# Attention reads and a cosine router in one kernel: the last seven expert blocks moved behind two run-time branches

## The chip, the cores and the metric

The kernel runs on one core of one Trainium2 chip. The metric is device time in microseconds (us) of one execution, median of the runs; all data is float32.

## What is computed

The reference has two parts. The first reads a batch of rows against a small set of states, both ways; the second sends every resulting row to the one expert whose embedding it resembles most.

```python
def _attn_ref(x, state):               # x (8, 8, 512, 64), state (8, 8, 32, 64)
    scores = scale * np.matmul(x, state.transpose(0, 1, 3, 2))
    ...
    xread = np.matmul(a, state)        # a: softmax of scores
    ...
    sread = np.matmul(a2, x)           # a2: softmax of scores the other way
    return np.concatenate([xread, sread], axis=2)

def _moe_ref(x, expert_emb, tau, w1, w2):   # x (4352, 512), 8 experts, F = 1024
    logits = xn @ en.T / tau                # xn, en: x and expert_emb by their lengths
    expert_idx = np.argmax(logits, axis=1)
    ...
    for e in range(E):
        mask = expert_idx == e
        ...
        h = np.maximum(x[mask] @ w1[e], 0.0)
        out[mask] = gate_w[mask, None] * (h @ w2[e])
```

The 8 x (512 + 32) = 4352 rows are 34 x 128. The inputs come from a fixed seed, so how many rows each expert gets is the same in every run.

## The kernel before

The work has three stages, one behind the other.

**First part (lines 89 to 344).** For each of 8 batches and 2 groups of heads TensorE computes scores and reads. Rows go to a buffer in DRAM, x_rows. Meanwhile SyncE's queue loads the first weights of all eight experts into SBUF, where they stay (w1_sb, 16 MB).

**The seam (lines 346 to 441).** The kernel puts the rows in blocks of 128 rows of one expert. An expert with n rows takes n / 128 blocks, rounded up; nb holds these numbers and b0 each expert's first block. With 4352 rows and 8 experts there are at least 34 blocks and at most 34 + 7 = 41 (NBLK). VectorE makes one-hot matrices (bm, oh, and rr with the row numbers; GpSimd makes the half of rr with the gates), and 34 matmuls (inv_ps, line 427) turn them into src_row and dst_row: which row stands at each place of each block, and where its result goes. An empty place reads row 0 and gets a destination past the end of the output, so that nothing is written for it. eblk is each block's expert.

**Second part, the expert stage (lines 443 to 542).** All 41 blocks run, whatever the counts are. A block j has these steps: `gather(j)`, an indirect DMA issued by GpSimd that fetches its 128 rows (xin, three buffers); `load_w2(j)`, a 2 MB load of the expert's second weights issued by SyncE (w2, two buffers); `turn_x`, four transposes on TensorE (xt_ps) and a copy on VectorE (xT); `hidden`, 8 matmuls against w1_sb (h_ps), with ReLU on ScalarE and VectorE; `turn_h`, eight transposes (ht_ps) and two copies (hT); `result`, 8 matmuls against w2 (y_ps), a multiplication by the gate on VectorE (y), and an indirect DMA on GpSimd that scatters the rows to the output. The profile counts two passes for each float32 matmul, hence 16 records for each of the two big steps. SyncE and TensorE read the block's expert into a register first (`expert`, line 446, a TENSOR_LOAD).

The order of the work is that of the loop, on each engine's own queue. It runs ahead: the hidden layer of the next block, the gather three blocks ahead, the second weights two blocks ahead.

```python
528    xin = {j: gather(j) for j in range(3)}
529    w2 = {j: load_w2(j) for j in range(2)}
530    xT = {j: turn_x(xin.pop(j)) for j in range(2)}
531    h = {0: hidden(0, xT.pop(0))}
532    for j in range(NBLK):
533        if j + 1 < NBLK:
534            h[j + 1] = hidden(j + 1, xT.pop(j + 1))
535        hT = turn_h(h.pop(j))
536        if j + 3 < NBLK:
537            xin[j + 3] = gather(j + 3)
538        if j + 2 < NBLK:
539            xT[j + 2] = turn_x(xin.pop(j + 2))
540        result(j, hT, w2.pop(j))
541        if j + 2 < NBLK:
542            w2[j + 2] = load_w2(j + 2)
```

In what follows h(j), y(j) and w2(j) are block j's hidden step, result step and second weights; blocks count from 0.

Of the kernel before, what the change touches and what calls it, by code (L numbers as in the profile page):

```python
# [10 lines left out]
I32 = mybir.dt.int32  # L11
AF = mybir.ActivationFunctionType
ALU = mybir.AluOpType
AX = mybir.AxisListType.X
PSUM = bass.MemoryType.PSUM
ROUND = 12582912.0  # 1.5 * 2**23: adding and subtracting it rounds to a whole number


@with_exitstack
def kernel(  # L20
# [10 lines left out]
    nc = tc.nc  # L31
    P = 128
# [4 lines left out]
    N = out.shape[0]  # L37
    R = S + Ns  # rows of one batch in the second part
    NCH = S // P  # row p * NCH + c of a batch sits in partition p, chunk c
    HG = 2  # groups of heads  # L40
    HPG = H // HG  # heads in a group: HPG * Ns = 128 rows of states
    GW = HPG * Dh  # features of a group
    XW = GW + E  # and the group's share of the logits behind them
    KD = D // P
    KF = F // P
    SCALE = float(Dh) ** -0.5
    NG = 2  # groups of batches: NCH slots a batch, and one for the group's state rows
    GB = B // NG
    SG = GB * NCH + 1
    NSLOT = NG * SG  # L50
    NBLK = N // P + E - 1  # blocks of 128 rows of one expert, at most
    BIG = 200000.0
# [37 lines left out]
    dst_row = pers.tile([P, NBLK], I32, name="dst_row")  # L90
    eblk = pers.tile([1, NBLK], I32, name="eblk")

    make_identity(nc, ident)

# [1 line left out]
    with ExitStack() as att_ctx:  # L96
# [24 lines left out]

        # Block diagonals of states, with the projections on the experts behind each group's.
        bdst = [att1.tile([P, HG, XW], FP32, name=f"bdst{i}") for i in range(2)]
        for t in bdst:
            nc.gpsimd.memset(t, 0.0)

        # Experts by their length and by tau, features in partitions.
        junk8 = att1.tile([P, D], FP32, tag="junk", name="junk8")[0:E]
# [11 lines left out]

        # What the routing needs that rests on shapes alone.
        nc.gpsimd.memset(ones, 1.0)
# [22 lines left out]
        def choose(s0, ns):  # L165
            """One-hot of each row's first greatest logit, and the counts of the slots before."""
            l = lg[:, s0 : s0 + ns]
            mx = lmax[:, s0 : s0 + ns]
            shp = [P, ns, E]
            sel = att1.tile([P, NCH, E], FP32, tag="sel", name="sel")[:, 0:ns]  # L170
            pm = att1.tile([P, NCH], FP32, tag="pm", name="pm")[:, 0:ns]
            nc.vector.tensor_reduce(mx.unsqueeze(2), l, axis=AX, op=ALU.max)
            nc.vector.tensor_tensor(sel, l, bc(mx, shp, 2), ALU.is_equal)
            nc.vector.tensor_tensor(sel, sel, bc(pref, shp, 1), ALU.mult)
            nc.vector.tensor_reduce(pm.unsqueeze(2), sel, axis=AX, op=ALU.max)
            nc.vector.tensor_tensor(eq[:, s0 : s0 + ns], sel, bc(pm, shp, 2), ALU.is_equal)
            for s in range(s0, s0 + ns):
                nc.gpsimd.tensor_tensor(cumx[:, s + 1], cumx[:, s], eq[:, s], ALU.add)

        def states(b):  # L180
            """The batch's states as block diagonals, as they are and transposed."""
            bs = bdst[b % 2]
            for i in range(HPG):
                nc.gpsimd.tensor_copy(
                    bs[Ns * i : Ns * i + Ns, :, Dh * i : Dh * i + Dh], st_nat[Ns * i : Ns * i + Ns, b]
                )
            ps = bank("st_ps")
            for g in range(HG):
                for j in range(2):
                    nc.tensor.transpose(  # L190
                        ps[:, (2 * g + j) * P : (2 * g + j + 1) * P], bs[:, g, j * P : j * P + P], ident
                    )
            bd = att.tile([P, HG, 2, P], FP32, tag="bd", name="bd")
            nc.scalar.activation(bd.rearrange("p g j n -> p (g j n)"), ps, AF.Copy)
            pp = bank("pj_ps")
            for g in range(HG):
                for j in range(2):
                    nc.tensor.matmul(  # L198
                        pp[:, g * E : g * E + E], lhsT=bd[:, g, j], rhs=enT[:, 2 * g + j],
                        start=(j == 0), stop=(j == 1),  # L200
                    )
            nc.vector.tensor_copy(
                bs[:, :, GW:XW], pp[:, 0 : HG * E].rearrange("p (g e) -> p g e", e=E)
            )
            return bs, bd

        def scores(b, g, xn, bd):
            """Scores of a group of heads both ways, and their exponentials."""
            xT = att.tile([P, 2, S], FP32, tag="xT", name="xT")
# [11 lines left out]
            for j in range(2):  # L221
                for c in range(NCH):
# [5 lines left out]
                    )  # L228
            # Over the rows: a state's scores lie in its partition.
            r2 = att.tile([P, 3], FP32, tag="r2", name="r2")  # L230
# [7 lines left out]
            nc.vector.tensor_scalar(dg, ident, r2[:, 2:3], None, ALU.mult)  # L238
            # Over the states of a head.
            nch = NCH * HPG  # L240
# [13 lines left out]
        def reads(b, g, xn, bs, xr, e1, e2, dg):  # L254
            """A group's columns of the batch's rows."""
            ps = bank("a_ps")
# [29 lines left out]
        def rows(b, xr):  # L286
            """Keep the batch's rows, and say where they go."""
            s0 = SG * (b // GB) + NCH * (b % GB)
            for g in range(HG):
                nc.sync.dma_start(  # L290
                    rows_by_batch[b, 0:S, g * GW : g * GW + GW].rearrange("(p c) d -> p c d", c=NCH),
                    xr[:, :, g, 0:GW],
                )
            nc.vector.tensor_tensor(lg[:, s0 : s0 + NCH], xr[:, :, 0, GW:XW], xr[:, :, 1, GW:XW], ALU.add)
            junk = att1.tile([P, D], FP32, tag="junk", name="junk")
            for c in range(NCH):
                nc.scalar.activation(
                    junk.rearrange("p (g d) -> p g d", g=HG), xr[:, c, :, 0:GW], AF.Square, accum_out=ssq[:, s0 + c : s0 + c + 1]
                )
            choose(s0, NCH)  # L300

        def state_rows(g):
            """The same for the states read in a group of batches."""
            s0 = SG * g + SG - 1
# [40 lines left out]

# [1 line left out]
    with tc.tile_pool(name="rt", bufs=1) as rt:  # L347
# [3 lines left out]

        # Gates: the greatest probability of each row.
        shp = [P, NSLOT, E]
# [11 lines left out]

        # A row's rank among its expert's, and the experts' counts behind them.
        nk = NSLOT * E
# [10 lines left out]
        def whole(dst, src, shift):  # L378
            """src / 128 up (shift > 0) or down to a whole number, of whole numbers src."""
            nc.vector.tensor_scalar(dst, src, 1.0 / P, shift, ALU.mult, ALU.add)  # L380
            nc.vector.tensor_scalar(dst, dst, ROUND, ROUND, ALU.add, ALU.subtract)

# [21 lines left out]

        # A block's expert: the last one that starts no later.
        shp = [1, NBLK, E]
# [5 lines left out]

        # Which row, with which gate, stands at each place of each block.
        shp = [P, NSLOT, NBLK]
# [19 lines left out]
        nc.vector.tensor_copy(gpos, inv[:, 1])  # L434
        # An empty place reads row 0, and is written nowhere.
        nc.vector.tensor_scalar(src_row, inv[:, 0], -1.0, 0.0, ALU.add, ALU.max)
# [4 lines left out]

# [1 line left out]
    moe = ctx.enter_context(tc.tile_pool(name="moe", bufs=2))  # L443
# [10 lines left out]
    def load_w2(j):  # L454
        t = moe.tile([P, KF, D], FP32, tag="w2", name="w2")
        ek = expert(j, mybir.EngineType.SP)
        nc.sync.dma_start(t, moe_w2[ds(ek, 1)].rearrange("o (k p) d -> p (o k) d", p=P))
        return t
# [68 lines left out]

    xin = {j: gather(j) for j in range(3)}
    w2 = {j: load_w2(j) for j in range(2)}
    xT = {j: turn_x(xin.pop(j)) for j in range(2)}  # L530
    h = {0: hidden(0, xT.pop(0))}
    for j in range(NBLK):
        if j + 1 < NBLK:
            h[j + 1] = hidden(j + 1, xT.pop(j + 1))
        hT = turn_h(h.pop(j))
        if j + 3 < NBLK:
            xin[j + 3] = gather(j + 3)
        if j + 2 < NBLK:
            xT[j + 2] = turn_x(xin.pop(j + 2))
        result(j, hT, w2.pop(j))  # L540
        if j + 2 < NBLK:
            w2[j + 2] = load_w2(j + 2)

# [29 lines left out]
```

## Time and profile before

| what | us |
|---|---|
| three timed runs | 885.47, 887.55, 893.33 |
| their median | 887.55 |
| profiled execution, first to last instruction (span) | 891.5 |

The span of the profiled execution lies between the timed runs; no device time of its own is listed for it. PE is TensorE's matmuls, PEld its weight loads, DVE is VectorE, ACT ScalarE, POOL GpSimd, SP SyncE; SPq and POOLq are the queues of the last two. L512 is line 512 of the kernel before. Times in the rows are us from the start of the span, unless marked ns.

### The profile page before, as it was taken

How to read it: one execution, taken by the hardware profiler on the slowest of the kernel's cores; microseconds unless marked ns; L12 is line 12 of the kernel's file. 1: busy time of each engine (PE TensorE's matmuls, PEld its weight loads, DVE VectorE, ACT ScalarE, POOL GpSimd, SP SyncE). 2: the span in 40 equal slices, each digit the busy share in tenths (PEclk: the TensorE clock that was granted, in tenths of full speed). 3: DMA queues.
4: the chain of work that ended last, by engine and by line, in shares of the span. 5: the costliest groups of instructions: out<-in, count | busy, mean ns of one | idle time of the engine just before them, and what ended most of it. 6: DMA issues, size and time to landing. Idle time of an engine off the chain costs nothing.

```text
span 891.5 us, 8858 instructions
## 1 busy us (share of the span) xinstructions
PE 830.0 (93%) x3280; PEld 467.8 (52%) x3280; DVE 234.2 (26%) x514; ACT 138.5 (16%) x280; POOL 125.0 (14%) x192
## 2 busy tenths in 40 slices
PE   6899999995659999999999999999999999999995
PEld 4677777774624444454545454444444454545442
DVE  3454556546211112121212121211111121212110
ACT  3343444443001000000000010101000000000000
POOL 2111111110120111111111111111111111110000
PEclk9899999997569999999999999999999999999998
DMA  9486844311073454555545464636464545545340
GB/s 269 156 285 189 260 130 95 72 49 60 0 248 103 144 195 159 176 178 161 193 149 198 136 207 132 215 132 219 134 204 145 186 168 171 174 154 188 123 163 0
DMA packets 97553, 140.84 MB, mean 158 GB/s; under 512 B 38174, under 2 KB 46366, under 8 KB 97512
## 3 DMA queue, kind: packets, MB, share of 16 engines
q1 hardware_dynamic: 90920, 120.59, 41.9%
q0 software_dynamic: 6560, 19.67, 6.6%
q8 instruction: 27, 0.44, 0.2%
q14 instruction: 14, 0.11, 0.0%
q10 hardware_dynamic: 32, 0.02, 0.0%
HBM read 122.44 MB, written 19.66 MB: 159 GB/s over the span
## 4 chain that ended last, share of the span: by engine, by line
issue 62%; PE 20%; POOL 10%; DVE 5%; DMA 2%; POOLq 1%; ACT 1%; DVEq 0%
PE sT_ps L218 5%; POOL out_dram L517 4%; POOL xin L462 4%; PE s_ps L223 3%; PE x_ps L270 3%; PE sr_ps L278 3%; PE inv_ps L427 2%; PE e_ps L263 1%; DVE xT L70 1%; PE pj_ps L198 1%; DMA xin<-x_rows,src_row 1%; PE a_ps L258 1%; DMA x_rows<-xs 1%; PE xt_ps L214 1%; PE st_ps L190 1%
## 5 line engine op out<-in xcount | busy, mean ns | idle before, releaser
L512 PE MATMUL y_ps<-w,hT 128*128 128x512 f32 x656 | 292.4, 599 | 0.6 <-ACT hT L68 0.6
L486 PE MATMUL h_ps<-w_sb,xT 128*128 x656 | 289.4, 594 | 0.0
L486 PEld LDWEIGHTS h_ps<-w_sb,xT 128*128 128x128 f32 x656 | 125.1, 191 | 157.3 <-issue 157.2
L512 PEld LDWEIGHTS y_ps<-w,hT 128*128 128x128 f32 x656 | 121.3, 190 | 142.2 <-issue 137.3
L494 ACT ACTIVATE h<-h_ps 128x512 f32<-128x512 f32 x41 | 24.5, 597 | 467.6 <-PE h_ps L486 467.6
L516 DVE TENSOR_SCALAR y<-y_ps,gpos 128x512 f32<-128x512 f32 x41 | 30.8, 751 | 250.6 <-PE y_ps L512 250.6
L496 DVE TENSOR_SCALAR h<-h_ps 128x512 f32<-128x512 f32 x41 | 28.4, 692 | 254.4 <-PE h_ps L486 254.4
L517 POOL DMA_INDIRECT out_dram<-y,dst_row x41 | 41.6, 1015 | 307.5 <-DVE y L516 307.5
L462 POOL DMA_INDIRECT xin<-x_rows,src_row x41 | 42.2, 1030 | 261.0 <-PE xt_ps L475 237.8
L505 PEld LDWEIGHTS ht_ps<-ident,h 128*128 128x128 f32 x328 | 38.3, 140 | 21.6 <-issue 21.6
L218 PE MATMUL sT_ps<-xT,bd 128*128 128x512 f32 x64 | 40.9, 772 | 7.4 <-DVE xT L70 7.2
L68 ACT ACTIVATE hT<-ht_ps 128x512 f32<-128x512 f32 x41 | 24.5, 597 | 138.6 <-PE ht_ps L505 138.6
L505 PE MATMUL ht_ps<-ident,h 128*128 128x128 f32 x328 | 42.5, 272 | 0.0
L223 PEld LDWEIGHTS s_ps<-bd,xT 128*128 128x128 f32 x256 | 33.1, 200 | 11.1 <-issue 11.1
L475 PE MATMUL xt_ps<-ident,xin 128*128 128x128 f32 x164 | 25.6, 280 | 9.9 <-DMA xin<-x_rows,src_row 9.9
L270 PE MATMUL x_ps<-bdst,aT 128*128 128x264 f32 x128 | 33.4, 405 | 0.0
L278 PEld LDWEIGHTS sr_ps<-xn,a 128*32 128x32 f32 x512 | 29.0, 110 | 5.5 <-DVE r L248 4.5
L278 PE MATMUL sr_ps<-xn,a 128*32 128x64 f32 x512 | 31.6, 220 | 0.0
L223 PE MATMUL s_ps<-bd,xT 128*128 128x64 f32 x256 | 31.4, 277 | 0.0
L477 DVE COPY xT<-xt_ps 128x512 f32<-128x512 f32 x41 | 27.9, 681 | 10.6 <-PE xt_ps L475 10.6
L70 DVE COPY hT<-ht_ps 128x512 f32<-128x512 f32 x41 | 28.4, 692 | 7.6 <-PE ht_ps L505 6.9
L427 PE MATMUL inv_ps<-rr,oh 128*128 128x82 f32 x68 | 14.8, 422 | 15.5 <-POOL rr L420 15.5
(127 smaller groups left out, 469.4 us busy)
## 6 DMA issues: line engine op xcount, KB each, us to landing
w<-in_moe_w_dram SPq DMA_DIRECT2D x41, 2048.0 KB, 10.1
w_sb<-in_moe_w_dram SPq DMA_DIRECT2D x8, 2048.0 KB, 9.7
xn<-in_x_dram SPq DMA_DIRECT2D x32, 256.0 KB, 4.8
x_rows<-xr SPq DMA_DIRECT2D x16, 512.0 KB, 4.4
xin<-x_rows,src_row POOLq DMA_INDIRECT x41, 3.7
out_dram<-y,dst_row POOLq DMA_INDIRECT x41, 7.8
st_nat<-in_state_dram SPq DMA_DIRECT2D x1, 512.0 KB, 4.7
x_rows<-xs SPq DMA_DIRECT2D x2, 256.0 KB
```

What stands on the lines that cost most here:

```text
L70: eng.tensor_copy(dst, src)
L218: nc.tensor.matmul(sT, lhsT=bd[:, g, j], rhs=xT[:, j], start=(j == 0), stop=(j == 1))
L223: nc.tensor.matmul(s[:, c * P + j * half : c * P + j * half + half], lhsT=xT[:, j, c * P : c * P + P], rhs=bd[:, g, j, j * half : j * half ...
L270: nc.tensor.matmul(ps[:, 0:XW], lhsT=aT[:, c * P : c * P + P], rhs=bs[:, g], start=True, stop=True)
L278: nc.tensor.matmul(ps[q0 : q0 + Ns, i * Dh : i * Dh + Dh], lhsT=a2[:, c * P + i * Ns : c * P + i * Ns + Ns], rhs=xn[:, c, (HPG * g + i) * ...
L427: nc.tensor.matmul(inv_ps[:, 0 : 2 * NBLK], lhsT=oh[:, s], rhs=rr[:, s].rearrange("p t k -> p (t k)"), start=(s == 0), stop=(s == NSLOT - 1),)
L462: nc.gpsimd.indirect_dma_start(out=t, out_offset=None, in_=x_rows[:], in_offset=bass.IndirectOffsetOnAxis(ap=src_row[:, j : j + 1], axis=0 ...
L486: nc.tensor.matmul(ps, lhsT=xT[:, k * P : k * P + P], rhs=w1f[:, ds(ek * (KD * F) + k * F + i * 512, 512)], start=(k == 0), stop=(k == KD ...
L505: nc.tensor.transpose(ps[:, k * P : k * P + P], h[:, f0 : f0 + P], ident)
L512: nc.tensor.matmul(ps, lhsT=hT[:, k * P : k * P + P], rhs=w2[:, k], start=(k == 0), stop=(k == KF - 1))
L516: nc.vector.tensor_scalar(y, ps, gpos[:, j : j + 1], None, ALU.mult)
L517: ins = nc.gpsimd.indirect_dma_start(out=out[:], out_offset=bass.IndirectOffsetOnAxis(ap=dst_row[:, j : j + 1], axis=0), in_=y, in_offset= ...
```

## The change

The loop of the expert stage becomes a function `run(a, z)` over blocks a to z - 1, with its own start (gathers, loads, first transposes) and its own end. It is called for blocks 0 to 33 unconditionally. Then every engine loads the number of blocks that hold rows, `count`, into a register and compares it with 34; if it is greater, blocks 34 to 36 run, and within that branch a second comparison with 37 guards blocks 37 to 40. `count` is one more VectorE instruction in the seam: first block of the last expert plus its number of blocks. Comments are dropped, so line numbers move (by 4 in the expert stage).

```diff
+    count = pers.tile([1, 1], I32, name="count")
...
         nc.vector.tensor_scalar(eblk, ne, -1.0, None, ALU.add)
 
-        # Which row, with which gate, stands at each place of each block.
+
+        nc.vector.tensor_tensor(count, b0[0:1, E - 1 : E], nb[0:1, E - 1 : E], ALU.add)
+
+
...
-    xin = {j: gather(j) for j in range(3)}
-    w2 = {j: load_w2(j) for j in range(2)}
-    xT = {j: turn_x(xin.pop(j)) for j in range(2)}
-    h = {0: hidden(0, xT.pop(0))}
-    for j in range(NBLK):
...
+    def run(a, z):
+
+        xin = {j: gather(j) for j in range(a, min(a + 3, z))}
+        w2 = {j: load_w2(j) for j in range(a, min(a + 2, z))}
+        xT = {j: turn_x(xin.pop(j)) for j in range(a, min(a + 2, z))}
+        h = {a: hidden(a, xT.pop(a))}
+        for j in range(a, z):
+            if j + 1 < z:
+                h[j + 1] = hidden(j + 1, xT.pop(j + 1))
+            hT = turn_h(h.pop(j))
+            if j + 3 < z:
+                xin[j + 3] = gather(j + 3)
+            if j + 2 < z:
+                xT[j + 2] = turn_x(xin.pop(j + 2))
+            result(j, hT, w2.pop(j))
+            if j + 2 < z:
+                w2[j + 2] = load_w2(j + 2)
+
+
+    always = N // P
+    more = always + (NBLK - always) // 2
+    run(0, always)
+    blocks = nc.values_load(
+        count[0:1, 0:1], min_val=always, max_val=NBLK,
+        skip_runtime_bounds_check_because="the sum over the experts of their rows / 128, rounded up",
+    )
+    with tc.If(blocks > always):
+        run(always, more)
+        with tc.If(blocks > more):
+            run(more, NBLK)
```

GpSimd's queue before, from the gather of block 34 to the scatter of block 33 (L462 is a gather, L517 a scatter; xin_3936 is block 34's rows, y_4074 block 33's result):

```order
L462 DMA xin_3936<-x_rows,src_row_77 128x512
L517 DMA out_0_dram<-y_3838,dst_row_78 4352x512
L462 DMA xin_3995<-x_rows,src_row_77 128x512
L517 DMA out_0_dram<-y_3897,dst_row_78 4352x512
L462 DMA xin_4054<-x_rows,src_row_77 128x512
L517 DMA out_0_dram<-y_3956,dst_row_78 4352x512
L462 DMA xin_4113<-x_rows,src_row_77 128x512
L517 DMA out_0_dram<-y_4015,dst_row_78 4352x512
L462 DMA xin_4172<-x_rows,src_row_77 128x512
L517 DMA out_0_dram<-y_4074,dst_row_78 4352x512
```

And the same queue now (L466 gathers, L521 scatters; y_4029 is block 33's result, xin_4042, xin_4046 and xin_4050 the rows of blocks 34, 35 and 36):

```order
L521 DMA out_0_dram<-y_4002,dst_row_78 4352x512
L521 DMA out_0_dram<-y_4029,dst_row_78 4352x512
L554 TENSOR_LOAD count_80
L558 COMPARE_AND_BRANCH
L466 DMA xin_4042<-x_rows,src_row_77 128x512
L466 DMA xin_4046<-x_rows,src_row_77 128x512
L466 DMA xin_4050<-x_rows,src_row_77 128x512
L521 DMA out_0_dram<-y_4139,dst_row_78 4352x512
L521 DMA out_0_dram<-y_4187,dst_row_78 4352x512
L521 DMA out_0_dram<-y_4214,dst_row_78 4352x512
L560 COMPARE_AND_BRANCH
```

Four gathers and four scatters stood between the gather of block 34 and the scatter of block 33; now that gather stands behind that scatter, a register load and a branch.

TensorE before, from the transposes of block 33's hidden rows on (ht_ps) to those of block 34's; between y_ps_4065 and the next ht_ps it reads block 35's expert and does that block's hidden matmuls:

```order
L505 MATMUL ht_ps_4042<-ident_61,h_3969 128x128 x4
L505 MATMUL ht_ps_4048<-ident_61,h_3969 128x128 x4
L475 MATMUL xt_ps_4058<-ident_61,xin_3995 128x128 x4
L512 MATMUL y_ps_4065<-w2_3961,hT_4041 128x512 x8
L446 TENSOR_LOAD eblk_79
```

TensorE now, from the result of block 32 on, over the first branch (w2_3959 belongs to block 33):

```order
L516 MATMUL y_ps_3993<-w2_3904,hT_3980 128x512 x8
L509 MATMUL ht_ps_4008<-ident_61,h_3967 128x128 x4
L509 MATMUL ht_ps_4014<-ident_61,h_3967 128x128 x4
L516 MATMUL y_ps_4020<-w2_3959,hT_4007 128x512 x8
L554 TENSOR_LOAD count_80
L558 COMPARE_AND_BRANCH
L479 MATMUL xt_ps_4064<-ident_61,xin_4042 128x128 x4
L479 MATMUL xt_ps_4071<-ident_61,xin_4046 128x128 x4
L450 TENSOR_LOAD eblk_79
```

The hidden layers of blocks 34 and 35 no longer stand between the results of blocks 32 and 33 and behind them: they wait for transposes of rows whose gathers stand behind block 33's scatter.

VectorE in the seam before, from the last small step before the one-hots on:

```order
L401 SCALAR_TENSOR_TENSOR low<-blk,dest 128x34
L418 TENSOR_TENSOR bm<-io,blk 128x1394
L362 TENSOR_REDUCE gate<-sh 128x34
L419 TENSOR_TENSOR rr<-bm,tok_69 128x34x41
L363 TENSOR_SCALAR gate<-gate 128x34
L424 TENSOR_TENSOR oh<-io,low 128x2176
L364 RECIPROCAL gate<-gate 128x34
L424 TENSOR_TENSOR oh<-io,low 128x2176
```

And now (line numbers one to four higher):

```order
L415 TENSOR_TENSOR count<-b_1950,nb 1x1
L381 TENSOR_SCALAR blk<-dest 128x34
L382 TENSOR_SCALAR blk<-blk 128x34
L363 TENSOR_REDUCE gate<-sh 128x34
L402 SCALAR_TENSOR_TENSOR low<-blk,dest 128x34
L422 TENSOR_TENSOR bm<-io,blk 128x1394
L364 TENSOR_SCALAR gate<-gate 128x34
L428 TENSOR_TENSOR oh<-io,low 128x2176
L365 RECIPROCAL gate<-gate 128x34
L423 TENSOR_TENSOR rr<-bm,tok_69 128x34x41
L428 TENSOR_TENSOR oh<-io,low 128x2176
```

The new instruction has shifted the scheduler's choice: the product of bm with the row numbers now stands behind the gate's reciprocal, not ahead of it.

A branch that is not gone into leads to a short piece of code that stands behind all the blocks: there each engine waits for what it has under way and adds to the semaphores what the blocks left out would have added, and GpSimd waits for its DMAs to land first.

## Rows read from the trace of the kernel before

**Rows 1.** The page: busy time of the engines, and granted TensorE clock in 40 slices.

```profile
span 891.5 us, 8858 instructions
PE 830.0 (93%) x3280; PEld 467.8 (52%) x3280; DVE 234.2 (26%) x514; ACT 138.5 (16%) x280; POOL 125.0 (14%) x192
PEclk9899999997569999999999999999999999999998
```

**Rows 2.** Two blocks by windows: start and end, length, busy time of each engine, clock.

```profile
700.00:715.17 15.17, 15.17 (x45) 7.37 (x44) 2.73 (x6) 1.19 (x2) 2.04 (x3) 1.00 0.51 173
715.17:730.34 15.17, 15.17 (x45) 7.37 (x44) 2.73 (x6) 1.19 (x2) 2.04 (x3) 1.00 0.51 173
```

**Rows 3.** DMA by queue (packets, MB) and scatters, 822 to 892 us.

```profile
q0 software_dynamic: 400, 0.06, 0.5%
...
out_dram<-y,dst_row POOLq DMA_INDIRECT x5, 6.9
```

**Rows 4.** Timeline, start of the expert stage: start, length, engine, instruction, [idle before].

```profile
248.30 1.26 POOL L462 DMA_INDIRECT xin<-x_rows,src_row  x1 [16.69 <-DVE dst_row L438]
249.87 1.00 POOL L462 DMA_INDIRECT xin<-x_rows,src_row  x1 [0.31 <-issue]
...
256.33 2.27 PE L475 MATMUL xt_ps<-ident,xin 128*128 128x128 f32 x8 [9.86 <-DMA xin<-x_rows,src_row]
258.39 15.24 PE L486 MATMUL h_ps<-w_sb,xT 128*128 x32
```

**Rows 5.** Timeline, end of the expert stage.

```profile
874.78 7.13 PE L512 MATMUL y_ps<-w,hT 128*128 128x512 f32 x16 [0.30 <-ACT hT L68]
881.95 0.75 DVE L516 TENSOR_SCALAR y<-y_ps,gpos 128x512 f32<-128x512 f32 x1 [6.34 <-PE y_ps L512]
882.98 0.98 POOL L517 DMA_INDIRECT out_dram<-y,dst_row  x1 [7.32 <-DVE y L516]
```

**Rows 6.** Lines L462 (gathers) and L517 (scatters), then DMA issues with median us to landing.

```profile
DMA to landing us min/median/max: 3.3/3.7/7.9
...
DMA to landing us min/median/max: 2.1/7.8/8.8
...
w<-in_moe_w_dram SPq DMA_DIRECT2D x41, 2048.0 KB, 10.1
```

**Rows 7.** Clock at the start of the expert stage, by windows.

```profile
256.33:258.39 2.06, 2.00 (x8) 1.54 (x9) 0.69 (x1) 0.00 (x0) 0.70 (x1) 0.50 1.04 408
258.39:261.20 2.81, 2.81 (x5) 1.26 (x5) 0.69 (x1) 0.00 (x0) 1.29 (x2) 0.53 1.05 388
261.20:273.50 12.30, 12.30 (x30) 5.31 (x30) 0.69 (x1) 1.19 (x2) 0.00 (x0) 1.00 0.30 113
```

**Rows 8.** Register loads of a block's expert: ns min, median, max.

```profile
L446 SPq TENSOR_LOAD <-eblk x41: 265/274/487, 220.3 to 843.7; - x41
L446 PEldq TENSOR_LOAD <-eblk x41: 295/299/497, 257.5 to 851.9; - x41
```

**Rows 9.** Timeline of the seam, VectorE, GpSimd and TensorE.

```profile
222.66 1.60 DVE L419 TENSOR_TENSOR rr<-bm,tok 128x1394 f32<-128x1394 f32 x1
224.18 0.17 DVE L363 TENSOR_SCALAR gate<-gate 128x34 f32<-128x34 f32 x1
...
226.60 0.36 DVE L364 RECIPROCAL gate<-gate 128x34 f32<-128x34 f32 x1
226.88 2.36 DVE L424 TENSOR_TENSOR oh<-io,low 128x2176 f32<-128x2176 f32 x1
227.18 4.44 POOL L420 TENSOR_TENSOR rr<-bm,gate 128x1394 f32<-128x1394 f32 x1 [13.25 <-DVE gate L364]
231.67 14.80 PE L427 MATMUL inv_ps<-rr,oh 128*128 128x82 f32 x68 [15.48 <-POOL rr L420]
```

**Rows 10.** The end of the program (L568), and the queue that brings instructions.

```profile
L568 POOLq DRAIN  x3: 40/107/7992, 882.7 to 891.3; - x3
...
q8 instruction: 27, 0.44, 0.2%
```

More of the change, by code (lines that the diff above doesn't have):

```diff
@@ L526, in result @@
         tc.add_to_no_dep_group("rows", ins.ins)
-    xin = {j: gather(j) for j in range(3)}
-    w2 = {j: load_w2(j) for j in range(2)}
-    xT = {j: turn_x(xin.pop(j)) for j in range(2)}
-    h = {0: hidden(0, xT.pop(0))}
-    for j in range(NBLK):
[L533 to L542, printed above, removed]
+    def run(a, z):
[25 more added lines that the diff above has]
+            run(more, NBLK)
 _INS = ["x", "state", "moe_expert_emb", "moe_tau", "moe_w1", "moe_w2"]
```

## The prediction

> **What bounds the kernel now.** The page comes first. TensorE's matmuls are busy for 830.0 of 891.5 us; no other engine passes 27% but the weight loads, which lie under the matmuls [rows 1]. So the question is how much TensorE work goes, and where TensorE will stand still. [...] The slices of the clock show one dip, 7 5 6, in the seam [rows 1]. From the timeline, the expert stage's matmuls run from the first hidden step at 258.39 [rows 4] to the end of the last result step, 874.78 + 7.13 = 881.91 [rows 5]. That is 623.52 us for 41 blocks; 41 x 15.17 would be 621.97. The 1.55 us left over are the start at a low clock and a last result step with less work in front of it.
>
> **How many blocks run.** The reference, on its own fixed inputs, sends 1599, 512, 64, 512, 581, 545, 512 and 27 rows to the eight experts. In blocks of 128, rounded up, that is 13 + 4 + 1 + 4 + 5 + 5 + 4 + 1 = 37. The trace agrees: from 822 us on, five scatters are issued, those of blocks 36 to 40, and the queue that carries them moves 0.06 MB, where five full blocks would be 5 x 128 x 2 KB = 1.31 MB [rows 3]. 27 rows of 2 KB are 0.055 MB: block 36 holds the last expert's 27 rows, and blocks 37 to 40 hold nothing. So `count` is 37: the first branch (37 > 34) is gone into, the second (37 > 37) is not. Four blocks go, and blocks 34 to 36 are started afresh.
>
> **What goes: four blocks.** 4 x 15.17 = 60.68 us of TensorE time [rows 2], all on the path, since nothing else stands beside it. Their gathers, 2 MB loads and empty scatters go too, at no gain: they were hidden under the matmuls.
>
> **What is added: one stop between blocks 33 and 34.** Let T be the end of y(33). Before, h(35) followed it with no gap, on rows gathered long ago. Now everything for block 34 begins behind the scatter of block 33 on GpSimd's queue, because that scatter waits for VectorE's y, which waits for T. Step by step:
> - From T to the end of that scatter's issue, read from the last block: result ends at 881.91, VectorE works 881.95 to 882.70, GpSimd issues 882.98 to 883.96, so T + 2.05 [rows 5].
> - Then GpSimd's register load of `count`, its branch, and the start of the gather. Two gathers in a row start 0.31 us apart from end to start [rows 4]. The load takes 0.27 to 0.30 us in the middle on the other two queues [rows 8]. A branch stands in no row. Its floor is nothing: load and branch need not wait for the issue to end, so 0.31 in all. For its ceiling I take one landing of the longest kind, 7.9, if code had to be brought [rows 6]. I take 1.25 in all, near the floor, since only sequencer steps are known to lie there: the gather starts at T + 3.3. [...]
> - The gather's landing. Alone it takes 3.7 us in the middle and 3.3 at least; the scatters, which are issued 1 us behind a 2 MB load, take 7.8; the first gather of the stage, behind two such loads, at most 7.9 [rows 6]. SyncE's queue isn't held up by its own branch: w2(35) is issued when y(33) lets its buffer go, at T, and lands about 10.1 us later [rows 6]. So the gather lies beside that load, as the scatters do. I take 7.1, so that it ends with the load at T + 10.4.
> - From the first transpose to the first hidden matmul: 258.39 - 256.33 = 2.06 us in the seam, with both blocks' transposes, the copy and the wait for the second gather in it [rows 4].
>
> Sum: 3.3 + 7.1 + 2.06 = 12.5 us from T to h(34). Ends: 2.05 + 0.31 + 3.3 + 2.06 = 7.7, and 2.05 + 7.9 + 7.9 + 2.06 = 19.9. To that come the 1.55 us of a start and an end, paid a second time. [...] The stop therefore costs 14.1.
>
> The other engines' loads and branches are free: TensorE, ScalarE and VectorE have nothing else to do until the gather lands. Buffers don't hold anything: all three row buffers are free by then, and w2(34) is loaded from the end of y(32) on, under y(33).
>
> **What the seam gains.** `count` is one tiny VectorE step, 0.2 us at most by its neighbours' 0.17 [rows 9]. But the order moved: the product of 1.60 us that stood ahead of the gate's sum, from 222.66 to the next start at 224.18, now stands behind the gate's reciprocal. GpSimd's part starts when that reciprocal is done, and the 34 matmuls when GpSimd's part is (231.62, 231.67) [rows 9]. So they begin 1.52 - 0.2 = 1.3 us sooner. VectorE's last one-hot then ends at about 229.4, still ahead of its use. Bounds: nothing, if the two engines get in each other's way with the new pairing, to 1.5. I take 1.3 off.
>
> **The end.** Block 36's scatter is followed by a jump past the code of four blocks and by waits that add to semaphores. Between the last scatter's start and the end of the span lie 8.5 us already, most of them GpSimd's closing DRAIN of 7.99 us [rows 5, 10]. The second branch on TensorE comes while y(36) runs, those of the others while they wait. I add 0.5; bounds 0, if all lies under what is there, and 4, if the DRAIN starts only when the scatter has landed and takes as long as now.
>
> **Sum.** 891.5 - 60.7 + 14.1 - 1.3 + 0.5 = 844.1 for the span, that is 47.4 less. The profiled execution's span is 4 us over the median of the timed runs, so I take the difference off the median: 887.55 - 47.4 = 840.1. Its own ends: stop 7.7 to 19.9, seam 0 to -1.5, end 0 to 4 give -53 to -35, or 835 to 852; most of that lies in 835 to 846.
>
> **Rivals.**
> - Branches cost code. Each engine's instructions come by DMA: 27 packets of 0.44 MB in all, 16 KB each, in this queue [rows 10]. If a branch makes the engine fetch its next code anew, GpSimd pays it at both branches with nothing beside it at the first, and TensorE's restart can come later than the gather. A landing of 3.3 to 7.9 us each [rows 6], say 5 for the first on the path and 5 at the end: 840.1 + 10 = 850. For it: the trace shows code arriving in pieces throughout. Against: the code of blocks 34 to 36 stands directly behind the branch, and the jump at the end lies beside the last scatter. [...]
> - A light stop. The gather isn't slowed by w2(35) and takes 3.7, and the branch hides under the scatter's issue: T to h(34) is 8.1, and the time 840.1 - 4.4 = 835.7. For it: the middle gather [rows 6]. Against: these are issued while no 2 MB load is on its way, and this one is.
> - The change doesn't do what it says: the kernel counts 38 or more. Then all 41 blocks run and the stop is paid twice: 887.55 + 28.2 - 1.3 + 0.5 = 915, slower. It is decided at one block more than 37, and three experts hold exactly 512 rows, so a single row that goes elsewhere could add a block. Against: the 0.06 MB of the last five scatters [rows 3], which come from the kernel's own routing.
>
> **Chances.** Forecast 0.72, code fetch 0.14, light stop 0.10, more blocks 0.04. A measurement of this kernel tells about 1%, some 9 us, from no change. The first three are all faster by over 3%; only the last is slower, by 3%. Nothing I see ends near no change, as four blocks less the stop would have to cancel, which needs a stop of some 60 us: 0.01 for that. The range takes in the light stop and the code fetch: 832 to 854.
>
> **What would show it.** Right: 592 result matmul records (37 x 16) where there were 656; one idle stretch of TensorE of 10 to 11 us near 774, ended by a gather, with the clock at half for some 3 us behind it; h(34) near 787; the 34 matmuls of the seam starting near 230.4; the span ending 9 to 11 us behind y(36). Wrong: 656 records (count over 37), a stop over 20 us or one ended by something other than the gather, or idle time of TensorE within blocks 0 to 33.

## The result, and the profile after

The changed kernel takes 844.76 us in the median of 4 runs (842.72 to 845.93), beside 889.78 us (885.47 to 893.33, 4 runs: the three known ones and one of 892.02) of the kernel before: a ratio of 0.9482, 95% interval 0.9442 to 0.9521. The forecast was 840.1 us with a range of 832 to 854. The profiled execution's span is 842.4 us, forecast 844.1.

The page of the changed kernel, busy time, clock in 40 slices, and the two big steps of a block:

```profile
span 842.4 us, 8400 instructions
PE 769.3 (91%) x3104; PEld 438.0 (52%) x3104; DVE 225.6 (27%) x499; ACT 133.7 (16%) x272; POOL 115.9 (14%) x184
PEclk9899999999559999999999999999999999999897
L516 PE MATMUL y_ps<-w,hT 128*128 128x512 f32 x592 | 263.9, 599 | 1.1 <-ACT hT L68 0.8
L490 PE MATMUL h_ps<-w_sb,xT 128*128 x592 | 262.6, 597 | 0.0
```

The same two steps on the page of the kernel before:

```profile
L512 PE MATMUL y_ps<-w,hT 128*128 128x512 f32 x656 | 292.4, 599 | 0.6 <-ACT hT L68 0.6
L486 PE MATMUL h_ps<-w_sb,xT 128*128 x656 | 289.4, 594 | 0.0
```

592 records are 37 x 16 where there were 41 x 16: four blocks are gone. The mean of a matmul, 599 and 597 ns for 599 and 594, is no shorter than before, so no block became cheaper. Beside the seam's dip, now 5 5, the clock has a second one (8) in the 38th of the 40 slices, from 779 to 800 us, which [rows 1] doesn't have. The 7 of the last slice is the end of the program.

The timeline between block 33 and block 34 (start, length, engine, instruction, idle before and what ended it):

```profile
764.16 7.13 PE L516 MATMUL y_ps<-w,hT 128*128 128x512 f32 x16 [0.30 <-ACT hT L68]
771.33 0.75 DVE L520 TENSOR_SCALAR y<-y_ps,gpos 128x512 f32<-128x512 f32 x1 [6.69 <-PE y_ps L516]
772.36 0.98 POOL L521 DMA_INDIRECT out_dram<-y,dst_row  x1 [7.32 <-DVE y L520]
773.65 1.05 POOL L466 DMA_INDIRECT xin<-x_rows,src_row  x1 [0.30 <-issue]
...
781.22 2.18 PE L479 MATMUL xt_ps<-ident,xin 128*128 128x128 f32 x8 [9.93 <-DMA xin<-x_rows,src_row]
783.19 15.23 PE L490 MATMUL h_ps<-w_sb,xT 128*128 x32
```

Read it from the top: the result of block 33 ends at 764.16 + 7.13 = 771.29, VectorE and the scatter follow, the gather of block 34 stands right behind the scatter's issue, and TensorE waits 9.93 us for its rows. From 771.29 to the hidden step are 11.90 us. That is the stop.

The clock there, by windows (start, end, length, PE busy, ..., PEclk, DMA share, GB/s):

```profile
771.29:773.65 2.36, 0.00 (x1) 0.00 (x0) 0.75 (x1) 0.00 (x0) 0.99 (x2) 1.00 0.48 141
773.65:781.22 7.57, 0.00 (x1) 0.01 (x1) 0.00 (x0) 0.00 (x0) 3.07 (x3) 0.62 0.99 361
781.22:783.19 1.97, 1.97 (x9) 1.50 (x9) 0.69 (x1) 0.00 (x0) 0.00 (x0) 0.50 0.29 109
783.19:787.00 3.81, 3.81 (x7) 1.67 (x7) 0.69 (x1) 0.00 (x0) 0.00 (x0) 0.66 0.02 4
```

While the gather is under way the DMA engines are full (0.99): w2(35) is on its way too. The granted clock falls during the idle time, from 1.00 until 775 us to 0.50 from 776 us on, and comes back within the first hidden matmuls: 0.53 in the mean from 783.19 to 785.9 us, 1.00 behind that.

In the seam (VectorE's reciprocal and the two steps behind it, GpSimd's product, the first of the 34 matmuls), beside [rows 9]:

```profile
222.44 0.36 DVE L365 RECIPROCAL gate<-gate 128x34 f32<-128x34 f32 x1
222.72 1.55 DVE L423 TENSOR_TENSOR rr<-bm,tok 128x1394 f32<-128x1394 f32 x1
223.03 3.63 POOL L424 TENSOR_TENSOR rr<-bm,gate 128x1394 f32<-128x1394 f32 x1 [11.42 <-DVE gate L365]
224.18 4.75 DVE L428 TENSOR_TENSOR oh<-io,low 128x2176 f32<-128x2176 f32 x1
226.70 14.80 PE L431 MATMUL inv_ps<-rr,oh 128*128 128x82 f32 x68 [13.46 <-POOL rr L424]
```

GpSimd's product starts when the reciprocal is done, as before, but takes 3.63 us where it took 4.44. The last one-hot takes 4.75 us where it took 2.36, and nobody waits for it.

At the end, GpSimd's queue at the second branch (L560: ns min, median, max; first and last start) and the closing lines (L587); L558 is its first branch and L554 its load of the count:

```profile
L560 POOLq EVENT_SEMAPHORE  x4: 17/43/2165, 831.2 to 831.4; - x4
...
L560 POOLq INC_SWDGE_SEM  x1: 1660/1660/1660, 833.6 to 833.6; - x1
...
L587 POOLq DRAIN  x3: 46/107/6107, 835.5 to 842.1; - x3
...
L558 POOLq COMPARE_BRANCH  x1: 40/40/40, 772.7 to 772.7; - x1
...
L554 POOLq TENSOR_LOAD <-count x1: 507/507/507, 772.1 to 772.1; - x1
```

The last result ends at 830.15, the span 12.25 us later; before it was 9.6 [rows 5, 10]. GpSimd waits for its last scatter to land (2.2 us), adds to its DMA semaphores (1.66 us), and only then starts the DRAIN with which it began at once before.

The parts against the forecast, in us of the two profiled executions:

| part | before | forecast | after |
|---|---|---|---|
| start to the compare of block starts (L409, now L410) | 217.72 | 217.72 | 215.19 |
| from there to the first of the 34 matmuls | 13.95 | 12.65 | 11.51 |
| from there to the first hidden step | 26.72 | 26.72 | 27.11 |
| first hidden step to the end of y(33), or of y(40) before | 623.52 | 517.33 | 517.48 |
| stop | none | 12.5 | 11.90 |
| h(34) to the end of y(36) | none | 47.06 | 46.96 |
| to the end of the span | 9.6 | 10.1 | 12.25 |

The first row isn't the change's: see the last section.

### The profile page after: what moved, and what is told of

Read it like the earlier page. It is cut to its first block, busy times and chain, and to the rows that moved or that the text cites. A ratio compares the mean times of both kernels' runs of the same rounds, so it can differ in the third digit from the quotient of the medians.

```text
span 842.4 us, 8400 instructions
## 1 busy us (share of the span) xinstructions
PE 769.3 (91%) x3104; PEld 438.0 (52%) x3104; DVE 225.6 (27%) x499; ACT 133.7 (16%) x272; POOL 115.9 (14%) x184
## 4 chain that ended last, share of the span: by engine, by line
PE 82%; issue 7%; DVE 5%; DMA 2%; POOL 1%; ACT 1%; POOLq 0%; ACTq 0%; DVEq 0%
PE y_ps L516 28%; PE h_ps L490 28%; PE sT_ps L219 5%; PE ht_ps L509 3%; PE s_ps L224 3%; PE x_ps L271 3%; PE sr_ps L279 3%; PE xt_ps L479 2%; PE inv_ps L431 2%; PE e_ps L264 2%; DVE xT L70 1%; PE pj_ps L199 1%; DMA xin<-x_rows,src_row 1%; PE a_ps L259 1%; DMA x_rows<-xs 1%
## 5 line engine op out<-in xcount | busy, mean ns | idle before, releaser
L516 PE MATMUL y_ps<-w,hT 128*128 128x512 f32 x592 | 263.9, 599 | 1.1 <-ACT hT L68 0.8
L490 PE MATMUL h_ps<-w_sb,xT 128*128 x592 | 262.6, 597 | 0.0
L490 PEld LDWEIGHTS h_ps<-w_sb,xT 128*128 128x128 f32 x592 | 113.4, 192 | 142.6 <-issue 142.3
L516 PEld LDWEIGHTS y_ps<-w,hT 128*128 128x128 f32 x592 | 109.4, 190 | 129.2 <-issue 123.9
L521 POOL DMA_INDIRECT out_dram<-y,dst_row x37 | 37.5, 1014 | 312.0 <-DVE y L520 304.7
L466 POOL DMA_INDIRECT xin<-x_rows,src_row x37 | 38.1, 1030 | 217.9 <-PE xt_ps L479 199.4
L509 PEld LDWEIGHTS ht_ps<-ident,h 128*128 128x128 f32 x296 | 34.6, 141 | 19.5 <-issue 19.5
L509 PE MATMUL ht_ps<-ident,h 128*128 128x128 f32 x296 | 38.4, 273 | 0.0
L479 PEld LDWEIGHTS xt_ps<-ident,xin 128*128 128x128 f32 x148 | 18.3, 150 | 22.0 <-DMA xin<-x_rows,src_row 11.4
L252 POOL TENSOR_TENSOR e<-e,r 128x512 f32<-128x512 f32 x16 | 16.8, 1048 | 78.3 <-DVE r L251 62.6
## 6 DMA issues: line engine op xcount, KB each, us to landing
w<-in_moe_w_dram SPq DMA_DIRECT2D x37, 2048.0 KB, 10.1
```

The source lines that it names most:

```text
L466: nc.gpsimd.indirect_dma_start(out=t, out_offset=None, in_=x_rows[:], in_offset=bass.IndirectOffsetOnAxis(ap=src_row[:, j : j + 1], axis=0 ...
L479: nc.tensor.transpose(ps[:, k * P : k * P + P], t[:, k * P : k * P + P], ident)
L490: nc.tensor.matmul(ps, lhsT=xT[:, k * P : k * P + P], rhs=w1f[:, ds(ek * (KD * F) + k * F + i * 512, 512)], start=(k == 0), stop=(k == KD ...
L509: nc.tensor.transpose(ps[:, k * P : k * P + P], h[:, f0 : f0 + P], ident)
L516: nc.tensor.matmul(ps, lhsT=hT[:, k * P : k * P + P], rhs=w2[:, k], start=(k == 0), stop=(k == KF - 1))
L521: ins = nc.gpsimd.indirect_dma_start(out=out[:], out_offset=bass.IndirectOffsetOnAxis(ap=dst_row[:, j : j + 1], axis=0), in_=y, in_offset= ...
```

## The experiments

The theory: the four blocks are worth 15.17 us each and nothing more; the stop is block 34's gather, which the branch keeps behind block 33's scatter on GpSimd's queue (it starts 0.30 us behind that scatter's issue); the branch itself costs next to nothing; the longer end is the catching up for the blocks left out. The rivals: branch, register loads or code to be brought make the stop, or starting the pipeline anew does. "Seam" in the table is the second row of the one above, "behind" the span less the first row, so that the first part's own scatter is left out.

| run | seam | stop | end | behind | time, ratio to before (95%) |
|---|---|---|---|---|---|
| before | 13.95 | none | 9.6 | 673.8 | |
| changed | 11.51 | 11.90 | 12.25 | 627.2 | 0.9482 (0.9442 to 0.9521) |
| e1, 37 blocks, no branch | 13.99 | none | 9.0 | 612.7 | 831.4, 0.9337 (0.9297 to 0.9376) |
| e2, two starts, no branch | 13.98 | 1.44 | 9.0 | 613.8 | 828.28, one run |
| e7, gathers ahead | 11.52 | 1.53 | 12.3 | 615.4 | 829.05, one run |
| e8, pipelined | 11.52 | 0 | 12.45 | 613.5 | 829.75, 0.9344 (0.9315 to 0.9373) |
| e3, both gone into | 11.52 | 12.04, 11.53 | 9.7 | 698.0 | 914.23, 1.0267 (1.0219 to 1.0315) |
| e4, skip in the middle | 11.52 | 18.58 | 9.0 | 631.6 | 846.47, one run |
| e5, one branch | 11.52 | 12.02 | 9.0 | 624.6 | 838.84, one run |
| e9, skip early | 11.52 | 1.15 and 0.72 | 9.0 | 613.6 | 828.76, 0.9310 (0.9278 to 0.9342) |
| e10, e8 again | 11.52 | 0 | 12.5 | 613.2 | 829.64, 0.9318 (0.9284 to 0.9351) |

**e1: 37 blocks in one loop.**

```diff
-    run(0, always)
...
-    with tc.If(blocks > always):
-        run(always, more)
-        with tc.If(blocks > more):
-            run(more, NBLK)
+    run(0, more)
```

> No branch: one loop over 37 blocks, as the kernel before but four blocks shorter; blocks 37 to 40, which hold no rows with these inputs, have no code. It gives what four blocks are worth without any stop. My theory (a block is 15.17 us of TensorE, nothing else goes): span 891.5 - 60.7 = 830.8 give or take 3, no idle stretch of TensorE behind the stage's start, 9.6 us from the last result matmul to the end. The seam's order is as before (the one-hots' product with the row numbers ahead of the gate's reciprocal, although the count is computed here too), so from the compare of block starts to the first of the 34 matmuls 14.0 to 14.2 us, not the 11.5 of the changed kernel. Rival (the skip's code makes the end longer only by being there; the 27 rows of the last scatter, not the skip, cost the 2.6 us at the end): 12.2 us at the end here too.

Measured: span 830.2, 9.0 us at the end, seam 13.99. The theory holds: the end is even shorter than the written 9.6, far from the rival's 12.2, so the last scatter's 27 rows are not what lengthens it. Behind the first part the kernel is 61.1 us shorter than before, 0.6 of them at the end; that leaves 60.5 for four blocks, forecast 60.7. The seam also corrects a sentence that stands ahead of the prediction. `count` is computed here too, yet VectorE's order is that of the kernel before:

```profile
222.51 1.60 DVE L423 TENSOR_TENSOR rr<-bm,tok 128x1394 f32<-128x1394 f32 x1
224.11 2.42 DVE L428 TENSOR_TENSOR oh<-io,low 128x2176 f32<-128x2176 f32 x1
226.45 0.36 DVE L365 RECIPROCAL gate<-gate 128x34 f32<-128x34 f32 x1
```

The product with the row numbers again stands ahead of the reciprocal. So the new instruction alone didn't move it: every kernel here with a branch has 11.5, both without, in which nothing reads `count`, have 14.0. Whether it is the branch or the register load ahead of it was not separated.

**e2: two starts without a branch.**

```diff
     run(0, always)
...
-    with tc.If(blocks > always):
-        run(always, more)
-        with tc.If(blocks > more):
-            run(more, NBLK)
+    run(always, more)
```

> Blocks 0 to 33 and 34 to 36 as two starts of the pipeline, as in the changed kernel, but without a branch; blocks 37 to 40, which hold no rows, have no code. Without the branch the scheduler puts the gathers of blocks 34 to 36 ahead of the last scatters again, though the two transposes and the hidden step of block 34 still stand behind the result of block 33. My theory (the stop of 11.9 us is the gather behind the scatter, not the restart): from the end of that result to the hidden step 1.2 to 2.2 us, the clock stays at 1.00, span some 832 to 833. Rival (the restart itself, with its loads and expert registers, is the stop): 8 us or more.

```profile
763.23 7.13 PE L516 MATMUL y_ps<-w,hT 128*128 128x512 f32 x16 [0.30 <-ACT hT L68]
770.20 1.04 PE L479 MATMUL xt_ps<-ident,xin 128*128 128x128 f32 x8
771.80 14.00 PE L490 MATMUL h_ps<-w_sb,xT 128*128 x32 [0.57 <-DVE xT L481]
```

The transposes follow the result with no idle time, the hidden step starts 1.44 us behind it, and the matmuls show no slow start: 1.04 us for the eight transposes and 14.00 for two hidden steps, where the changed kernel has 2.18 and 15.23. Starting the pipeline anew is cheap; the gather's place is what costs. The span came out lower than written, 826.5, because the first part ended 5 us earlier than in the kernel before.

**e7: the gathers ahead of the branch.**

```diff
             if j + 3 < z:
                 xin[j + 3] = gather(j + 3)
+            elif j + 3 < more and z == always:
+                ahead[j + 3] = gather(j + 3, "xin_ahead", 3)
...
-    run(0, always)
+    ahead = run(0, always)
...
     with tc.If(blocks > always):
-        run(always, more)
+        run(always, more, ahead)
```

> The changed kernel with both branches, but the gathers of blocks 34 to 36 are issued ahead of the first branch, in the loop over blocks 0 to 33, into three row buffers of their own. My theory (the stop is the gather that stands behind the scatter of block 33): the branch stays, the stop shrinks from 11.9 to 1.2 to 2.2 us, and the half clock behind it goes, so the span is 842.4 - 10 - 1.3 = 831 give or take 3. Rival (the register loads, branches and code behind them are the stop): it stays above 8 us, span about 841.

```profile
760.43 7.13 PE L516 MATMUL y_ps<-w,hT 128*128 128x512 f32 x16 [0.30 <-ACT hT L68]
767.40 1.04 PE L479 MATMUL xt_ps<-ident,xin 128*128 128x128 f32 x8
769.09 14.00 PE L490 MATMUL h_ps<-w_sb,xT 128*128 x32 [0.65 <-DVE xT L481]
```

Both branches are there, and the stop is 1.53 us. That settles it against the branch, the loads and the code behind it: 10.4 of the 11.9 us were the gather. The transposes take 1.04 us and two hidden steps 14.00, as in e2, so the slow start behind the stop is gone with it. Its span of 827.1 lies at the written range's lower side, again by an early first part.

**e8: pipelined over the branch.** In the loop over blocks 0 to 33 the look-ahead runs on to block 36; what is carried over the branch has buffers of its own.

```diff
             if j + 1 < z:
                 h[j + 1] = hidden(j + 1, xT.pop(j + 1))
+            elif j + 1 < more:
+                kept[2][j + 1] = hidden(j + 1, xT.pop(j + 1), "h_ahead", 1)
...
+            elif j + 3 < more:
+                kept[0][j + 3] = gather(j + 3, "xin_ahead", 1)
...
+            elif j + 2 < more:
+                kept[1][j + 2] = turn_x(xin.pop(j + 2), "xT_ahead", 1)
...
-    run(0, always)
+    kept = run(0, always, more)
...
-        run(always, more)
+        run(always, more, 0, kept)
```

> The changed kernel with both branches, but the loop over blocks 0 to 33 also gathers blocks 34 to 36, transposes the rows of 34 and 35 and does the hidden step of block 34, all ahead of the first branch, with buffers of their own for what is carried over; within the branch the loop goes on where it was. My theory: TensorE reads the count and branches while the result step of block 33 still runs, so the stop goes altogether: 0 to 0.5 us, span 842.4 - 13.4 = 829 give or take 3, 0.93 of the kernel before, 0.984 of the changed one. Rival (a branch costs TensorE a stop whatever stands ready): 2 us or more at the first branch.

```profile
769.56 7.13 PE L516 MATMUL y_ps<-w,hT 128*128 128x512 f32 x16
776.53 7.03 PE L490 MATMUL h_ps<-w_sb,xT 128*128 x16
```

The hidden step of block 35 starts before the modelled end of the result ahead of it, as in any block [rows 2]: TensorE doesn't notice the branch. The version beats both kernels, 0.9344 of the one before (0.9315 to 0.9373), and unlike e1 it is written for any count; only 37 was run. With a count of 34 it would do a hidden step of some 7 us for nothing. Against e1, which fits these inputs alone, it loses 3.4 us at the end and gains 2.5 in the seam.

**e3: both branches gone into.** The second comparison is made with 36.

```diff
-        with tc.If(blocks > more):
+        with tc.If(blocks > more - 1):
```

> The changed kernel with the second comparison against 36 in place of 37, so that with a count of 37 both branches are gone into and all 41 blocks run, the last four empty. This is the forecast's slower rival, priced. My theory: a second stop as long as the first (11.9 us and some 1.5 of low clock and a start over), and no skip at the end: span 842.4 + 60.7 + 13.4 - 2.6 = 914, about 1.03 of the kernel before. Rival (the first stop is long for reasons of that place, such as a first run through new code): a second stop under 8 us, span 908 or less.

```profile
822.59 7.13 PE L516 MATMUL y_ps<-w,hT 128*128 128x512 f32 x16 [0.30 <-ACT hT L68]
...
838.83 1.11 PE L479 MATMUL xt_ps<-ident,xin 128*128 128x128 f32 x4 [9.11 <-DMA xin<-x_rows,src_row]
...
841.25 8.94 PE L490 MATMUL h_ps<-w_sb,xT 128*128 x18
```

The second stop, from 829.72 to 841.25, is 11.53 us, the first 12.04. At 914.23 us the kernel is 2.7% slower than before: this is the forecast's slower rival (915), and its price was about right. The change pays with these inputs; a count above 37 would run the same instructions, and by this run it wouldn't pay.

**e4: the skip in the middle.**

```diff
-    with tc.If(blocks > always):
-        run(always, more)
-        with tc.If(blocks > more):
-            run(more, NBLK)
+    with tc.If(blocks > more):
+        run(more, NBLK)
+    run(always, more)
```

> The same blocks as in the changed kernel, but the branch that is not gone into (blocks 37 to 40) stands between blocks 33 and 34, and blocks 34 to 36 run unconditionally behind it. It prices a skip in the middle of the work. My theory (a skip costs what its catching up waits for: GpSimd waits for all its DMAs to land, then adds to their semaphores, 1.66 us in the changed kernel, before the next gather): the scatter of block 33 lands about 9 us behind the result, the gather starts 10.5 to 11.5 behind it instead of 2.4, and the stop is 16 to 18 us; span 842.4 + 5 - 2.6 = 845. Rival (code beyond the skip has to be brought, several us on each engine): the gather starts more than 14 us behind the result, the stop over 20 us.

```profile
762.55 7.13 PE L516 MATMUL y_ps<-w,hT 128*128 128x512 f32 x16 [0.30 <-ACT hT L68]
786.38 1.94 PE L479 MATMUL xt_ps<-ident,xin 128*128 128x128 f32 x8 [16.70 <-DMA xin<-x_rows,src_row]
788.26 12.26 PE L490 MATMUL h_ps<-w_sb,xT 128*128 x24
...
781.51 1.05 POOL L466 DMA_INDIRECT xin<-x_rows,src_row  x1 [9.79 <-DMA out_dram<-y,dst_row]
...
769.80 1.37 SPq L461 DMA_DIRECT2D w<-in_moe_w_dram  x2
...
L558 POOLq EVENT_SEMAPHORE  x4: 17/43/7515, 771.3 to 779.0; - x4
...
L558 PEldq COMPARE_BRANCH  x1: 3840/3840/3840, 763.5 to 763.5; - x1
...
L558 POOLq INC_SWDGE_SEM  x1: 1539/1539/1539, 779.1 to 779.1; - x1
```

The mechanism is the written one: 7.5 us until the scatter has landed, 1.54 for the semaphores, then the gather, 11.83 us behind the result. Both sizes lie a little over the written ones, the gather by 0.3 us, the stop of 18.58 by 0.6. What I had not written: both second-weight loads are issued only at 769.80, behind the end of the result at 769.68 and beside TensorE's catching up (769.7 to 769.9); that SyncE waits for what this adds is my reading. And TensorE's jump took 3.84 us, the one sign of the code-fetch rival in any run; it ended at 767.3, under block 33's result step. What the jump waited for is not shown, and in e9 TensorE's jump over the same four blocks took 0.35 us.

**e5: one branch.**

```diff
     with tc.If(blocks > always):
         run(always, more)
-        with tc.If(blocks > more):
-            run(more, NBLK)
```

> The changed kernel without its second branch; blocks 37 to 40, which hold no rows, have no code. My theory (the end is 2.6 us longer than before because of the skip: GpSimd waits for its scatters to land and adds to semaphores before its closing DRAIN can begin): 9.4 to 10 us from the last result matmul to the end, the stop still 11.9, span 839.8 give or take 3. Rival (it is the last scatter, which carries 27 rows here and none before): 12 us again.

```profile
820.93 7.13 PE L516 MATMUL y_ps<-w,hT 128*128 128x512 f32 x16 [0.30 <-ACT hT L68]
...
L585 POOLq DRAIN  x3: 40/113/7181, 829.1 to 836.8; - x3
```

9.0 us from 828.06 to the end, the stop still 12.02. The longer end is the skip's, 3.2 us by this pair; I had written 9.4 to 10.

**e9: the skip moved ahead of blocks 34 to 36, in the pipelined version (the diff is against e8); e10: that version unchanged, beside it.**

```diff
     with tc.If(blocks > always):
-        run(always, more, 0, kept)
         with tc.If(blocks > more):
             run(more, NBLK)
+        run(always, more, 0, kept)
```

> The pipelined version (blocks 34 to 36 prepared ahead of the first branch) with the skip of blocks 37 to 40 moved from the end to the place right behind the first branch, ahead of the rest of blocks 34 to 36, whose rows, transposes and first hidden step are ready by then. My theory (the skip's price is GpSimd's wait for its DMAs, 1.5 to 1.7 us of adding to semaphores and the late closing DRAIN; ahead of three blocks' matmuls it lies under them): 9.0 us from the last result matmul to the end in place of 12.4, TensorE stands still for under 0.6 us at the skip, span 827.8 - 3 = 825 give or take 3, 0.996 of the pipelined version. Rival (the jump of 3.8 us seen on TensorE's queue, or the catching up, stops TensorE there): 3 us or more of idle time at the skip, no gain.

> The pipelined version once more, unchanged, beside the one with the early skip on the same chip: 0.934 of the kernel before, 12.4 us from the last result matmul to the end.

```profile
769.49 7.13 PE L516 MATMUL y_ps<-w,hT 128*128 128x512 f32 x16
777.77 7.11 PE L490 MATMUL h_ps<-w_sb,xT 128*128 x16 [1.15 <-DVEq L572]
...
786.91 7.11 PE L516 MATMUL y_ps<-w,hT 128*128 128x512 f32 x16 [0.72 <-DMA w<-in_moe_w_dram]
```

A miss. The end is 9.0 us as written, but TensorE stands still for 1.15 us at the skip (its own catching up stands at 776.7 to 776.8, behind the result's end at 776.62, and VectorE's, which releases the hidden step by the trace, at 777.6) and 0.72 us for w2(34), which I take to be issued late as in e4. From the start of y(33) to the end of y(36) it takes 48.0 us, 2.2 more than e8's 45.8, against 3.4 gained at the end. The 1.2 left don't show in the whole: the intervals of e9 and e10 cover each other's values, and behind the first part they take 613.6 and 613.2 us.

## Why the prediction was right, and where it was off

**Bound and count.** TensorE bounds the kernel, a block is 15.17 us [rows 2], four go: the stretch to the end of y(33) was 517.48 for 517.33 forecast. The 0.06 MB of the last five scatters [rows 3] gave the count, and 592 records confirm it.

**The stop.** 11.90 for 12.5. Its terms: to the end of the scatter's issue 2.05, as forecast. Load and branch: 0.31 instead of 1.25; on GpSimd's queue the load takes 0.51 us from 772.1 and the branch 0.04 at 772.7, both done before the scatter's issue ends at 773.34, so the floor was right. The landing: 7.57 instead of 7.1, beside w2(35) as argued. Transposes to hidden step: 1.97 for 2.06. The clock fell to 0.50 and came back 2.7 us into the hidden matmuls, as in the seam, where it was 2.8 [rows 7]. e7 and e2 show that the gather's place was the mechanism; by the lengths of their matmuls the clock's fall goes with it.

**The seam.** Right in sign, mis-sized: 2.44 us for 1.3. The reciprocal came 1.63 us sooner, and 0.81 is GpSimd's product, which the forecast took at the 4.44 us that it had before. The rows suggest that this was no length of its own: it ends 2.38 us behind the end of the VectorE step that it meets, before as after (229.24 to 231.62 [rows 9], 224.27 to 226.66), and in all eleven traces within 0.02 us. It met the one-hot before and meets the shorter, earlier product now, and the ends of these two, counted from the compare of block starts, lie the 2.44 us apart. That `count` alone moved the order was wrong (e1).

**The end.** Mis-sized: 2.6 us for 0.5, inside its bounds of 0 to 4: the skip's 3.2 (e5), less 0.6 because the last block now has rows (e1). I had named the case, a DRAIN that starts only when the scatter has landed, and then taken it for the unlikely end.

**The number.** The span was off by 1.7 us: first part -2.5, seam -1.1, stop -0.6, end +2.1, the rest +0.4. Without the first part, which the change doesn't touch, the terms were 0.8 us too low in sum; that -1.7 of seam and stop stands against +2.5 of the others is luck. The time was off by 4.7. Taking the difference off the median was sound, since the chance in the first part stands in both terms of that difference and cancels. But the median of three runs was low: the fourth moved it from 887.55 to 889.78, by 2.2 us. The 1.6 us left lie within the spread of the runs. A span is not a time, though: the execution with a span of 842.4 took 844.45 us, and a later one of the kernel before with a span of 891.5 took 893.24. So the profiled execution of before was at the slow end of its runs.

**The rivals.** Code fetch: not on the path in any run. The light stop: no, the gather did meet the load, with the DMA engines 0.99 busy; in e4, where it starts with most of the two loads through (some 3.5 MB moved from 769.68 to 781.5 us, at 272 and 399 GB/s), it lands in 4.87 us (781.51 to 786.38). More blocks: not with these inputs, but e3 shows the price. The chances as written, with the 0.01 for no change, add up to 1.01.

## What to carry to other kernels

A run-time branch that was gone into cost an engine's queue 0.3 to 0.6 us of load and compare here (0.33 on SyncE's, 0.60 on VectorE's in the changed kernel), mostly under other work; what cost 12 us was the work behind it on the same queues, which could no longer be issued ahead. So let the look-ahead run across the branch, with buffers of its own for what is carried, and expect a skip to cost its catching up, here a wait for the DMAs in flight (2.2 us at the end, 7.5 in e4) and 1.5 to 1.7 us of GpSimd's. To learn how much of a data-dependent loop is empty, read the bytes that its last transfers moved; it works where, as here, the empty blocks come last and write nothing.

## What the runs showed that I had not expected

The first part, which no kernel here changes, ended between 211.7 and 217.7 us in the eleven profiled executions. Two of them by windows of the first 100 us, the kernel before and e7; the eighth number is the granted clock:

```profile
0.00:100.00 100.00, 84.91 (x599) 66.81 (x600) 47.52 (x138) 39.24 (x84) 19.30 (x66) 0.95 0.73 212
```

```profile
0.00:100.00 100.00, 84.90 (x640) 68.87 (x640) 50.34 (x146) 40.75 (x87) 20.22 (x67) 0.98 0.77 227
```

At 0.95 TensorE got through 599 matmuls, at 0.98 through 640, in the same busy time. That is 7% more matmuls for 3% more clock, so the clock alone doesn't account for it, and whether it is the cause is not shown. The 6 us lie between executions of different kernels; runs of the kernel before differ by 8. Of the one kernel profiled twice, e8 and e10, the spans are 2.9 us apart and the first parts 3.2. What sets the clock in that stage was not tried.

GpSimd's product and VectorE's steps in the seam seem to take turns. The product ends 2.38 us behind the VectorE step that it meets, and in the changed kernel the one-hot of 4.75 us, which starts while the product runs, ends 2.27 us behind the product's end (226.66 to 228.93), close to the 2.36 that it takes in the kernel before. This reads as each waiting until the other is done; no run took one of them alone, so it is not shown. And the end is 9.6 to 9.7 us when the last block is empty (before, e3), 9.0 when it has rows and nothing is skipped behind it.
